# Transposing keys, queries and outputs by DMA from pair 8 on, in an attention and mixture-of-experts kernel on one core

## The chip, the cores and the metric

The kernel runs on one core of one Trainium2 chip. The metric is the device time of one execution in microseconds, as a median over runs. Engines are called as in the profile: PE is the matrix engine (PEld its weight loads), DVE the vector engine, ACT the scalar engine, POOL the GpSimd engine, and SP the engine that only issues DMAs and waits for them. A name with a q behind it (SPq, POOLq) is the engine's instruction queue. Every engine works through its own instructions in the order in which the program wrote them; between engines only semaphores order the work.

## The reference

Inputs are q, k and v of 4 batches, 8 heads, 768 positions and 64 elements, and the weights of a mixture of 8 experts (512 to 1024 to 512). The attention of one head, and then the experts on all 3072 rows:

```python
k_sum = k.reshape(B, H, nb, 32, D).max(axis=3)
v_sum = v.reshape(B, H, nb, 32, D).mean(axis=3)
scores_l = where(|pos_q - pos_k| < 16, scale * q @ k.T, -1e9)
scores_s = scale * q @ k_sum.T + log(32)
a = softmax(concatenate([scores_l, scores_s]))
attn = a @ concatenate([v, v_sum])            # heads are put side by side: x is 3072 x 512
P = exp(x @ w_gate - max); 8 times: P /= rows; P /= columns; P *= N / E
out = sum over e of P[:, e] * (relu(x @ w1[e]) @ w2[e])
```

## The kernel before, in words

**Pairs.** Two heads are worked on together. There are 16 such pairs, four to a batch, so that pair i belongs to batch i // 4. The four pairs of batch 0 are cut into two halves of 384 positions (pair_half); pairs 4 to 15 are taken whole (pair_whole). The steps of a whole pair, with the functions that do them, are:

- `load_qk`, `load_v` on POOL: two DMAs for k, two for q, one for v, cast from float32 to bfloat16 on the way, into the buffers kst, qst and vx. Each has six buffers (NQ), so the load of pair i waits until pair i - 6 has been read.
- The transposes of keys and queries. `tr` does them on PE, six 128x128 blocks for k and six for q, into a PSUM bank (tile tkq), and `tr_out` copies the bank to kT or qT on ACT or DVE. `tr_dma` does each with one DMA transpose from SP instead, from kst or qst straight into kT or qT. kT and qT have four buffers (NB): pair i overwrites those of pair i - 4 and has to wait for its last readers.
- `key_max` on DVE (lines 375 to 378, tiles kh, km, ksT): the largest key of each block of 32.
- `block_sums` on PE and `block_out` on DVE (tiles vs, Ve): the block means of v. `near_values`: four small DMAs from SP that put the rows at the edges of the 128-row tiles into Ve.
- `scores` on PE (tile sg), `score_exp` on ACT (er), `masks` (em) and `edges` (Ee) on DVE, `summaries` on PE (ss) and `summary_exp` on ACT, `values` on PE (av), `normalize` on DVE (rc, xs).
- The output's transpose into xT, the experts' input: `to_xT` on PE (six blocks, tile tx) with `x_out` as its copy on ACT or DVE, or `x_dma`, one DMA transpose from SP.

In the kernel before, pairs 4 to 11 have keys and queries transposed on PE and pairs 12 to 15 by DMA; outputs of pairs 10 to 14 go by DMA and the others on PE.

**The work beside it.** Expert 0 is done in plain form, half a batch (384 rows) at a time, while attention still runs: `hidden0` (tile hps, eight tiles of four matmuls each, one for each of the four pairs of the batch) and `project0` (tile yps, three row blocks in two parts). `expert0` of a batch needs the xT of that batch's four pairs. For the first half of batch 0 the first BEGUN = 2 hidden tiles are started with three of the four pairs, and the fourth matmul follows when its pair is there. After attention come experts 1 to 7 in a form with seven products instead of eight (lines 930 to 1125), 84 groups that repeat with a fixed period.

**Who sets the order.** Class Plan simulates all engines from costs and delays written in the code, and the instructions are emitted in the order of that simulation. A unit has an engine or several to choose from, a cost, dependences, a priority (smaller is more urgent; attention has 20 + i, expert 0 has 1000 and up) and a `lag`, the time that the plan allows after the unit's end before its readers can start, used for DMAs. At each step the plan takes, on each engine, the unit that could start first, and among those that could start within 0.02 us the most urgent one. Nothing is put in order again at run time: where the plan has put an instruction whose input comes late, its engine waits, and all that the plan put behind it waits too. The plan's PSUM banks are rings: three of tag m (expert 0), one double bank s (scores), three of tag a (the rest of attention).

`bridge` begins the second stage. It writes zeros into two PSUM banks with dummy matmuls (tile allg, three in the kernel before) and adds the row and column scalings of P to the plan.

Of the kernel before, what the change touches and what calls it, by code (L numbers as in the profile page):

```python
# [136 lines left out]
def kernel(  # L137
# [12 lines left out]
    B, H, S, D = q.shape  # L150
# [4 lines left out]
    KD = DM // 128  # L155
# [3 lines left out]
    PB = H // 2  # L159
# [76 lines left out]
    NB = PB  # L236
    NE = 2
    NS = 1
    NA = 3
    BEGUN = 2  # L240
    ctx.enter_context(tc.manual_schedule())
    first = ExitStack()
    wfirst = first.enter_context(tc.tile_pool(name="wfirst", bufs=1, side="right"))
# [4 lines left out]
    if True:  # L248
# [6 lines left out]
        kT = [attn.tile([128, S], BF16, name=f"kT{i}") for i in range(NB)]  # L255
# [318 lines left out]
                in_=at.pop(("lp", b)), func=AF.Exp, bias=0.0, scale=1.0 / XS)  # L574

        def hidden0(key, t0, f, dks):
            if f == 0 and 0 in dks:
                at["h", key] = hpool.tile([128, KF, HS], FP16, tag="h", name="h")
            if 0 in dks:
                at["hp", key, f] = bank("m", "hps")  # L580
            hidden_mm(0, at["hp", key, f], t0, HS, f, dks)
# [106 lines left out]
        def pair_start(i, prio):  # L688
            o = i - NB
            war_k = [U.get(("S", o, 0)), U.get(("S", o, 1)), U.get(("km", o))]  # L690
            war_q = war_k[:2] + [U.get(("ss", o, 0)), U.get(("ss", o, 1))]
            tag = "m" if i < PB else "a"
            for z in range(2 if i >= PB else 1):
                if i >= 12:
                    U["tr", i, z] = U["kT", i, z] = add("SP", 1.25, lambda z=z: tr_dma(i, z),
                                                        [U["kq"[z], i]] + (war_k, war_q)[z], prio, lag=5.5)
                    continue
                buf = Buffer(tag)
                U["tr", i, z] = add("PE", 0.5 if i < PB else 0.335, lambda z=z: tr(i, z, tag),
                                    [U["kq"[z], i], U["ident"]] + (war_k, war_q)[z]  # L700
                                    + [U["tr", i, 0] if z else U.get(("S", i - 1, 1 if i > PB else 0))],
                                    prio, opens=[buf], shape="col" if i < PB else None)
                U["kT", i, z] = add({"ACT": 0.8} if z == 0 else {"ACT": 0.8, "DVE": 0.95},
                                    0, lambda z=z: tr_out(U["kT", i, z].on, i, z), [U["tr", i, z]], prio,
                                    uses=[buf])
            if i < PB:
                query_half(i, 0, prio)
            U["km", i] = add("DVE", 0.85, lambda: key_max(i), [U["kT", i, 0]] + war_q[2:], prio)
            if i == 0:
                U["gc"] = add("DVE", 0.35, gate_constants, [U["km", 0]], 0.5)  # L710
            buf = Buffer("a")
            U["vs", i] = add("PE", 0.345, lambda: block_sums(i),
                             [U["v", i]] + ([U.get(("A", i - NE, 1))] if i >= PB else []), prio + 0.01, opens=[buf])
            U["Vs", i] = add("DVE", 0.24 if i < PB else 0.7, lambda: block_out(i), [U["vs", i]],
                             prio + 0.01, uses=[buf])
# [39 lines left out]

        def pair_whole(i, prio):
            U["near", i] = add("SP", 2.5, lambda: near_values(i), [U["v", i], U.get(("A", i - NE, 1))], prio,
                               lag=4.5)
            for h in range(2):
                buf = Buffer("s")  # L760
                U["S", i, h] = add("PE", 0.215, lambda h=h: scores(i, h),
                                   [U["kT", i, 0], U["kT", i, 1], U.get(("ed", i - 2))], prio, opens=[buf], shape="row")
                U["X", i, h] = add("ACT", 0.97, lambda h=h: score_exp(i, h), [U["S", i, h]], prio, uses=[buf])
                U["mk", i, h] = add("DVE", 0.56, lambda h=h: masks(i, h),
                                    [U["X", i, h], U.get(("A", i - 2, 1))], prio)
            U["ed", i] = add("DVE", 0.78, lambda: edges(i),
                             [U["X", i, 0], U["X", i, 1], U["mk", i, 1], U.get(("A", i - NE, 1))], prio)
            for h in range(2):
                buf = Buffer("a")
                U["ss", i, h] = add("PE", 0.17, lambda h=h: summaries(i, h, "a"),  # L770
                                    [U["km", i], U["kT", i, 1], U.get(("A", i - NE, 1))], prio, opens=[buf])
                U["sx", i, h] = add("ACT", 0.46, lambda h=h: summary_exp(i, h), [U["ss", i, h]], prio, uses=[buf])
            for h in range(2):
                buf = Buffer("a")
                U["A", i, h] = add("PE", 0.36, lambda h=h: values(i, h),
                                   [U["mk", i, h], U["ed", i], U["sx", i, h], U["Vs", i], U["near", i]],
                                   prio, opens=[buf])
                U["no", i, h] = add("DVE", 0.68, lambda h=h: normalize(i, h),
                                    [U["A", i, h], U.get(("xt", i - 2))], prio, uses=[buf])
            if 10 <= i < 15:  # L780
                U["xt", i] = U["x", i] = add("SP", 1.25, lambda: x_dma(i), [U["no", i, 0], U["no", i, 1]], prio,
                                             lag=6.5)
            else:
                buf = Buffer("a")
                U["xt", i] = add("PE", 0.34, lambda: to_xT(i), [U["no", i, 0], U["no", i, 1]], prio, opens=[buf])
                U["x", i] = add({"ACT": 0.8, "DVE": 0.9}, 0, lambda: x_out(U["x", i].on, i), [U["xt", i]], prio,
                                uses=[buf])

        halves, zero = [], []
# [1 line left out]
        def expert0(t0, xs):  # L791
            key, n = t0, len(halves)
            halves.append(key)
            pr = 1000.0 + n
            w = [U["w1", i] for i in range(2)]
            evac, old = [], [U.get(("pj", halves[n - 2], c)) for c in range(HG)] if n >= 2 else []
            for f in range(KF):
                buf = Buffer("m")

                k = KD - 1 if t0 == 0 and f < BEGUN else 0  # L800
                if k:
                    b = add("PE", 0.162 * k, lambda f=f, k=k: hidden0(key, t0, f, range(k)), xs[0:k] + [w[0]],
                            pr + f * 0.01, opens=[buf])
                    zero.append(b)
                m = U["hd", key, f] = add("PE", 0.65 - 0.162 * k, lambda f=f, k=k: hidden0(key, t0, f, range(k, KD)),
                                          xs + [w[f // 4]] + old + ([b] if k else []), pr + f * 0.01,
                                          **{"uses" if k else "opens": [buf]})

                def ev(f=f):
                    relu(U["rl", key, f].on, at["h", key][:, f, 0:HS], at.pop(("hp", key, f))[:, 0:HS])  # L810
                U["rl", key, f] = add({"ACT": 0.5, "DVE": 0.56}, 0, ev, [m], -1.0, uses=[buf])
                evac.append(U["rl", key, f])
                zero.extend([m, evac[-1]])
            for c in range(HG):
                buf = Buffer("m")
                p0 = add("PE", 0.866, lambda c=c: project0(key, c, 0), evac[0:4] + (U["w2d"] if t0 >= N // 2 else [U["w2"]]),
                         pr + 0.1 + c * 0.02, opens=[buf])
                p1 = add("PE", 0.866, lambda c=c: project0(key, c, 1), evac[4:8] + [p0],
                         pr + 0.11 + c * 0.02, uses=[buf])
                U["pj", key, c] = p1  # L820

                def ev(c=c):
                    copy(U["yo", key, c].on, out_acc[:, t0 // 128 + c, :], at.pop(("yp", key, c))[:])
                U["yo", key, c] = add({"ACT": 0.58, "DVE": 0.68}, 0, ev, [p1], -1.0, uses=[buf])
                zero.extend([p0, p1, U["yo", key, c]])
# [55 lines left out]
                expert0(b * S, xs)  # L881
                expert0(b * S + HS, xs)
        def hold():
            for r in range(12 % NB, NB):
                nc.gpsimd.tensor_copy(out=held[0:1, 0:1], in_=qT[r][0:1, W:W + 1])

        def hold_near():
# [27 lines left out]
    if True:  # L915
# [253 lines left out]

        def bridge():  # L1170
            t = [fps.tile([128, 512], FP32, tag="g", name="allg", bufs=2) for _ in range(2)]
            for n in (0, 1, 0):
                nc.tensor.matmul(t[n][:], lhsT=zeros[:], rhs=zeros[:, None, :].to_broadcast([128, 4, 128]),
                                 start=True, stop=True)
            plan.more({"ab": 2, "g": 2, "k": 1, "c5": 1, "c2": 1})
# [194 lines left out]
```

## Time and profile before

| what | value |
|---|---|
| median of 3 runs | 670.95 us (670.42 to 671.23) |
| the profiled execution | 669.62 us |
| its span, first to last instruction | 667.9 us |
| mean granted clock of PE | 0.999 |
| busy shares PE, PEld, DVE, ACT, POOL | 99%, 65%, 87%, 60%, 20% |
| DMA transposes: xT, kT, qT | 5, 4, 4 |
| PE matmuls of 128x128 transposes: tkq of whole pairs, tx | 96, 66 |

Rows of the groups give busy time and the mean duration of one instruction. The ends of matmuls are modelled and matmuls overlap, so what one more matmul costs PE is read from the distance between the starts of neighbours, not from the duration. A DMA's row on a queue is its issue; its landing is told apart. Attention lies in the first 115 us, expert 0 ends at about 164 us, and the 84 groups take the rest.

### The profile page before, as it was taken

To read this page: it belongs to the slowest core of one execution; us is meant where nothing else is said; L and a number is where in the kernel's file an instruction comes from. 1 tells how busy PE (TensorE), PEld (TensorE's weight loads), DVE (VectorE), ACT (ScalarE), POOL (GpSimd) and SP (SyncE) were. 2 spreads that over 40 slices of the span, in tenths; PEclk is the share of its full clock that TensorE was granted. 3 is DMA by queue.
4 is the path that set the end of the run, shared out by engine and by line. 5 is a ranking of instruction groups with operands and counts; after the bars stand their busy time and mean duration, and the time that the engine had idled before them with its cause. 6 is when DMAs were issued, how large, how long until landed. Compare 5 with 4: busy or idle time off the path is not lost.

```text
span 667.9 us, 13518 instructions
## 1 busy us (share of the span) xinstructions
PE 659.0 (99%) x5077; PEld 435.7 (65%) x5077; DVE 582.2 (87%) x1475; ACT 399.7 (60%) x782; POOL 131.8 (20%) x179
## 2 busy tenths in 40 slices
PE   8999999999999999999999999999999999999996
PEld 4766656555666666666666666666666666666665
DVE  8889998785999988998799978998899889998885
ACT  6777676566777765555555555555555555555551
POOL 8699404223011010201010000101020101100001
PEclk9999999999999999999999999999999999999999
DMA  9999939500513050503231051306040233201224
GB/s 162 184 154 147 148 72 95 71 1 8 73 17 32 1 80 1 49 1 55 26 33 17 0 80 17 33 1 79 1 47 3 39 41 29 20 1 64 79 80 158
DMA packets 124033, 36.75 MB, mean 55 GB/s; under 512 B 110144, under 2 KB 121152, under 8 KB 123968
## 3 DMA queue, kind: packets, MB, share of 16 engines
q0 software_dynamic: 104128, 25.93, 41.2%
q1 hardware_dynamic: 18880, 9.22, 6.1%
q8 instruction: 40, 0.66, 0.4%
q10 hardware_dynamic: 960, 0.74, 0.3%
q14 instruction: 25, 0.20, 0.1%
HBM read 52.45 MB, written 6.29 MB: 88 GB/s over the span
## 4 chain that ended last, share of the span: by engine, by line
PE 89%; DVE 7%; DMA 1%; ACT 1%; issue 1%; ACTq 0%; DVEq 0%
PE xy L989 37%; PE pg L983 16%; PE pa L983 11%; PE pb L983 11%; PE yps L231 5%; PE hps L221 5%; DVE xs L547 1%; DMA kT<-kst 1%; PE sg L383 1%; PE tkq L349 1%; DVE em L435 1%; DVE km L377 1%; DVE h L214 0%; DVE kh L375 0%; PE tx L554 0%
## 5 line engine op out<-in xcount | busy, mean ns | idle before, releaser
L989 PEld LDWEIGHTS <-hf 128*128 128x128 f16 x2352 | 230.1, 98 | 95.8 <-issue 0.8
L989 PE MATMUL xy<-w,hf 128*128 128x256 f16 x1312 | 183.4, 273 | 0.0
L989 PE MATMUL xy<-ws,hf 128*128 128x256 f16 x984 | 147.6, 273 | 0.1
L212 ACT ACTIVATE hf<-pg 128x512 f16<-128x512 f32 x84 | 50.1, 597 | 151.3 <-PE pg L983 151.2
L1125 DVE SCALAR_TENSOR_TENSOR out_acc<-xy,P_sb,out_acc 128x512 f32<-128x512 f32 x164 | 115.1, 744 | 2.1 <-PE xy L989 2.1
L930 DVE TENSOR_TENSOR hf<-hf 128x512 f16<-128x512 f16 x252 | 100.3, 425 | 8.9 <-DVE hf L933 0.5
L983 PE MATMUL pa<-xT,w 128*128 128x512 f16 x336 | 99.9, 379 | 0.0
L983 PEld LDWEIGHTS <-w 128*128 128x128 f16 x672 | 65.8, 98 | 43.5
L933 DVE TENSOR_TENSOR hf<-pb,c 128x512 f16<-128x512 f32 x84 | 58.1, 692 | 36.7 <-PE pb L983 34.4
L197 POOL DMA_DIRECT2D w<-in_moe_w_dram x56 | 41.8, 758 | 219.9 <-PE pg L983 191.7
L983 PEld LDWEIGHTS <-ws 128*128 128x128 f16 x504 | 49.3, 98 | 25.1
L1017 ACT COPY c<-pg 128x512 f32<-128x512 f32 x84 | 49.2, 585 | 22.4 <-PE pg L983 22.4
L933 DVE TENSOR_TENSOR hf<-pg,c 128x512 f16<-128x512 f32 x84 | 57.1, 680 | 0.7 <-PE pg L983 0.7
L212 ACT ACTIVATE hf<-pa 128x512 f16<-128x512 f32 x84 | 50.6, 603 | 0.9 <-PE pa L983 0.9
L1002 ACT COPY pg<-pa 128x512 f32<-128x512 f32 x84 | 47.9, 570 | 4.9
L983 PE MATMUL pg<-xT,w 128*128 128x512 f16 x168 | 50.0, 379 | 0.0
L983 PE MATMUL pg<-xTs,w 128*128 128x512 f16 x168 | 50.0, 379 | 0.0
L983 PE MATMUL pb<-xTs,ws 128*128 128x512 f16 x168 | 50.0, 379 | 0.0
L983 PE MATMUL pb<-xT,ws 128*128 128x512 f16 x168 | 50.0, 379 | 0.0
L983 PE MATMUL pg<-xTs,ws 128*128 128x512 f16 x168 | 50.0, 379 | 0.0
L1010 ACT COPY c<-pb 128x512 f32<-128x512 f32 x84 | 49.8, 593 | 0.0
L221 PE MATMUL hps<-xT,w 128*128 128x384 f16 x256 | 48.9, 326 | 0.0
(152 smaller groups left out, 827.5 us busy)
## 6 DMA issues: line engine op xcount, KB each, us to landing
w<-in_moe_w_dram POOLq DMA_DIRECT2D x8, 1024.0 KB, 9.0
w<-in_moe_w_dram POOLq DMA_DIRECT2D x56, 128.0 KB, 3.5
out_dram<-out_acc SPq DMA_DIRECT2D x20, 256.0 KB, 2.0
vx<-in_v_dram POOLq DMA_DIRECT2D x16, 192.0 KB, 5.9
qst<-in_q_dram POOLq DMA_DIRECT2D x31, 96.0 KB, 5.2
kst<-in_k_dram POOLq DMA_DIRECT2D x24, 96.0 KB, 5.4
w<-in_moe_w_dram POOLq DMA_DIRECT2D x2, 512.0 KB, 8.8
Ve<-vx SPq DMA_DIRECT2D x48, 10.2 KB, 4.0
```

The source lines that it names most:

```text
L197: nc.gpsimd.dma_start(out=t[:, :, h, :], in_=moe_w1[e].rearrange("(dk p) f -> p dk f", p=128)[:, :, f:f + 128])
L212: nc.scalar.activation(out=out, in_=in_, func=AF.Relu, bias=0.0, scale=1.0)
L221: nc.tensor.matmul(hp[:, 0:n], lhsT=w1s[e][:, dk, 128 * f:128 * (f + 1)], rhs=xT[:, dk, t0:t0 + n], start=(dk == 0), stop=(dk == KD - 1))
L231: nc.tensor.matmul(yp[:], lhsT=h[:, f, c * 128:(c + 1) * 128], rhs=w2s[e][:, f, :], start=(f == 0), stop=(f == KF - 1))
L930: nc.vector.tensor_tensor(out=out, in0=in0, in1=in1, op=ALU.subtract)
L933: nc.vector.tensor_tensor(out=out, in0=in0, in1=in1, op=ALU.add)
L983: nc.tensor.matmul(bank[:], lhsT=w[:, dk, :], rhs=x[:, dk, :], start=start and dk == 0, stop=dk == KH - 1, skip_group_check=True)
L989: nc.tensor.matmul(bank, lhsT=a(f)[:, 128 * c:128 * (c + 1)], rhs=w[:, f, :], start=start and f == 0, stop=f == FH - 1, skip_group_check=True)
L1002: nc.scalar.copy(out=B["g"][:], in_=B["a"][:])
L1010: nc.scalar.copy(out=B["c5"][:], in_=B["b"][:])
L1017: nc.scalar.copy(out=B["c2"][:], in_=B["g"][:])
L1125: nc.vector.scalar_tensor_tensor(out=acc, in0=src, scalar=P_sb[:, t, e:e + 1], in1=acc, op0=ALU.mult, op1=ALU.add)
```

## The change

Two constants are new, QKD = 8 and XD = 8: keys and queries are transposed by DMA from pair 8 on (12 before), and outputs of pairs 8 to 14 (10 to 14 before). The plan's delays for these DMAs and for the small DMAs of `near_values` now depend on the pair, and the plan's cost of a copy from PSUM by DVE is 0.57 us instead of 0.95 and 0.9; the copy of a whole pair's kT may now go to DVE as well. The first two hidden tiles of batch 1 are begun with three pairs, as those of batch 0 are, and the tile h is taken when the last of the four matmuls is written. `bridge` writes two dummy matmuls. `hold` reads the same four qT buffers as before, since 12 % NB is 0.

```diff
+    QKD = 8
+    XD = 8
...
         def hidden0(key, t0, f, dks):
-            if f == 0 and 0 in dks:
+            if KD - 1 in dks and ("h", key) not in at:
                 at["h", key] = hpool.tile([128, KF, HS], FP16, tag="h", name="h")
...
-                if i >= 12:
+                if i >= QKD:
                     U["tr", i, z] = U["kT", i, z] = add("SP", 1.25, lambda z=z: tr_dma(i, z),
-                                                        [U["kq"[z], i]] + (war_k, war_q)[z], prio, lag=5.5)
+                                                        [U["kq"[z], i]] + (war_k, war_q)[z], prio, lag=6.0 if i < 14 else 3.0)
                     continue
...
-                U["kT", i, z] = add({"ACT": 0.8} if z == 0 else {"ACT": 0.8, "DVE": 0.95},
+                U["kT", i, z] = add({"ACT": 0.8} if i < PB else {"ACT": 0.8, "DVE": 0.57},
                                     0, lambda z=z: tr_out(U["kT", i, z].on, i, z), [U["tr", i, z]], prio,
                                     uses=[buf])
...
             U["near", i] = add("SP", 2.5, lambda: near_values(i), [U["v", i], U.get(("A", i - NE, 1))], prio,
-                               lag=4.5)
+                               lag=4.5 if i < 13 else 3.0)
...
-            if 10 <= i < 15:
+            if XD <= i < 15:
                 U["xt", i] = U["x", i] = add("SP", 1.25, lambda: x_dma(i), [U["no", i, 0], U["no", i, 1]], prio,
-                                             lag=6.5)
+                                             lag=3.0 if 9 < i < 13 else 6.5)
             else:
                 buf = Buffer("a")
                 U["xt", i] = add("PE", 0.34, lambda: to_xT(i), [U["no", i, 0], U["no", i, 1]], prio, opens=[buf])
-                U["x", i] = add({"ACT": 0.8, "DVE": 0.9}, 0, lambda: x_out(U["x", i].on, i), [U["xt", i]], prio,
+                U["x", i] = add({"ACT": 0.8, "DVE": 0.57}, 0, lambda: x_out(U["x", i].on, i), [U["xt", i]], prio,
                                 uses=[buf])
...
-                k = KD - 1 if t0 == 0 and f < BEGUN else 0
+                k = KD - 1 if t0 in (0, S) and f < BEGUN else 0
...
-            for r in range(12 % NB, NB):
+            for r in range(NB):
                 nc.gpsimd.tensor_copy(out=held[0:1, 0:1], in_=qT[r][0:1, W:W + 1])
...
-            for n in (0, 1, 0):
+            for n in range(2):
                 nc.tensor.matmul(t[n][:], lhsT=zeros[:], rhs=zeros[:, None, :].to_broadcast([128, 4, 128]),
                                  start=True, stop=True)
```

## The prediction

> **What bounds the kernel now.** I read the page first (busy shares), then the engines' busy time by stretch, then the timeline of the pairs that change, then the DMA landings and the waits.
>
> ```profile
> PE 659.0 (99%) x5077; PEld 435.7 (65%) x5077; DVE 582.2 (87%) x1475; ACT 399.7 (60%) x782; POOL 131.8 (20%) x179
> ```
>
> ```profile
> core 0: us, PE busy (x) PEld busy (x) DVE busy (x) ACT busy (x) POOL busy (x), PEclk, DMA share, GB/s
> 25.00:45.00 20.00, 20.00 (x269) 13.54 (x268) 16.11 (x51) 14.99 (x27) 16.23 (x20) 1.00 2.26 159
> 45.00:65.00 20.00, 19.63 (x233) 13.05 (x231) 18.24 (x55) 14.04 (x23) 19.88 (x25) 1.00 2.28 149
> 65.00:85.00 20.00, 19.97 (x230) 12.79 (x228) 18.30 (x57) 14.30 (x25) 9.91 (x13) 1.00 1.87 143
> 85.00:105.00 20.00, 19.49 (x194) 11.00 (x193) 18.87 (x60) 14.85 (x26) 0.87 (x3) 1.00 0.35 66
> ```
>
> From 25 us to the end PE has work at nearly every moment, at the full clock; in 45 to 105 us it idles 0.37 + 0.03 + 0.51 = 0.91 us. Attention is not the bound: where it waits, PE does expert 0, of which some 49 us are left when attention ends at 115 us. So the time is the sum of PE's work, and work taken off PE shortens it, as long as PE never has to wait in its fixed order. DVE stands at 91 to 94% in 45 to 105 us and sets attention's pace. The DMA share of about 2.3 means that more than two packets per engine are in flight until 85 us.
>
> **What is removed.** PE's timeline shows pair 8's transposes and the matmuls behind them:
>
> ```profile
> 60.06 0.50 PE L349 MATMUL tkq<-ident,kst 128*128 128x128 bf16 x6
> 60.40 0.50 PE L349 MATMUL tkq<-ident,qst 128*128 128x128 bf16 x6
> 60.73 0.51 PE L393 MATMUL vs<-vx,m_blk 128*128 128x128 bf16 x6
> ```
>
> From start to start six blocks take 0.34 and 0.33 us, so 0.335; the durations of 0.50 overlap the neighbour. Eight such units go (pairs 8 to 11, at 60.06, 60.40, 64.63, 64.97, 71.38, 74.11, 81.57 and 81.91): 8 x 0.335 = 2.68 us. Two output transposes go (pair 8 at 71.83, next start 72.16; pair 9 at 80.01, next start 80.55, of which about 0.2 is a stall): 2 x 0.335 = 0.67 us. One dummy of 512 columns goes: three of 379 ns cover 0.8 us together, so a further one costs (0.81 - 0.38) / 2 = 0.216 us. It lies behind attention, where PE is full. The sum is 2.68 + 0.67 + 0.22 = 3.57 us.
>
> The Trainium skill ("VectorE: DVE Perf Modes", Rules for kernel authors) speaks against the change: a 128x128 transpose belongs on TensorE where PSUM is a fit destination, and on the DMA crossbar otherwise. Its table there gives 390 ns on TensorE and 1309 ns by DMA; by those the 60 blocks would free 23.4 us of PE (an estimate from that page), while the starts above show 56 ns for a block in a row of blocks, so the trace decides for 3.57.
>
> Off PE, the copies of these banks go: DVE copied qT of pairs 8 to 11 (0.55 us each, 2.2 us), ACT copied the four kT and two xT (0.80 each, 4.8 us). That is worth nothing in itself, but DVE is nearly full there, so attention can run up to 2.2 us ahead.
>
> **What is added.** Ten DMA transposes from SP.
>
> ```profile
> L354 SPq DMA_TRANSPOSE kT<-kst x4: 1210/1224/1323, 65.5 to 88.8; - x4
> L354 SPq DMA_TRANSPOSE qT<-qst x4: 1214/1243/1923, 67.7 to 90.2; - x4
> DMA to landing us min/median/max: 2.7/5.4/7.4
> ```
>
> *On SP*: ten issues of 1.24 us, 12.4 us in 46 to 85 us, beside 2.5 us for a pair's four small DMAs. That is about 5.0 us a pair (6.2 with the output) against a pair's pace of 6 to 7 us: it fits, but behind a transpose that waits for its load stand the small DMAs of the next pair, and `values` waits for those.
>
> *Landing*: 2.7 us when the DMAs are quiet, 7.0 to 7.4 us beside loads (pairs 12 and 13). The plan allows 1.25 + 6.0 = 7.25. They are issued early: k and q of pair 8 are loaded at about 46 and 47 us, so kT of pair 8 can land at about 54 us, while PE's route gave it at 61.4 us (copy at 60.60 + 0.80). The reuse of kst by the load of pair 14 (issued at 65.7) is still after that. The outputs of pairs 8 and 9 would be issued at about 71.8 and 80.3 us, when their `normalize` ends, and by the dearest row have landed by 79.2 and 87.7; the first to wait for that, `normalize` of pairs 10 and 11, came at 84.26 and 91.65.
>
> *On the DMA engines*: in the backlog after the w2 load v of pairs 4 and 5 landed at 32.50 and 36.33, so the five loads of a pair took 3.83 us, against 4.25 us between issues on POOL, so there is a spare tenth. A transpose occupies all engines for about 1.4 us when alone. Four pairs times 2.8 us plus two outputs are some 14 us more in a stretch that has little room; loads of pairs 10 to 13 will land 3 to 8 us later than the plan believes, which counts no DMA time for transposes.
>
> *The wait*: `key_max` on DVE is the first reader, and the plan puts it where it thinks the keys land, not where they are needed. This is shown already, for pair 12, whose scores come only at 88.5 us:
>
> ```profile
> 72.95 0.36 DVE L375 TENSOR_TENSOR kh<-kT 128x384 bf16<-128x384 bf16 x1 [0.71 <-DMA kT<-kst]
> ```
>
> DVE stood 0.71 us there with masks, normalisations and copies behind it, and PE lost almost nothing (0.03 us idle in that whole 20 us stretch). For the new stalls of PE I bound from below by -0.9 us (all of today's idle in 45 to 105 us vanishes) and from above by +6 us (DVE waits out most of an 8 us lateness, with some cover). I take +0.5, nearest to the row of pair 12.
>
> The two begun tiles: six matmuls of hps are moved, not added (162 ns each from start to start, 0.97 us). They matter at 61.9 to 65.9 us. There PE has run out of batch 0's expert work and batch 1 waits for pair 7's output (copied at 64.42 to 65.22); 1.34 us of the removed transposes lay just there, as filling. The begun tiles and pair 8's scores, ready earlier, take their place. If both failed, 1.34 us would be given back. The same gap threatens at 104 us, when batch 2 starts: pair 11's output lands at 97.50, but the plan believed 94.77 + 1.25 + 6.5 = 102.5. With a lag of 3.0 it is 99.0, so that end is loosened as far as PE moves up.
>
> **The sum.** The profiled span 667.9 - 3.57 + 0.5 = 664.8 us; with the 1.7 us around it 666.5, against 669.62, so -3.07. The median of the runs stands 1.33 us above the profiled execution: 670.95 - 3.07 = 667.9 us. About 0.2% (1.3 us) is what a measurement can tell from no change.
>
> **Rivals.**
>
> *Late keys stop DVE (slower).* The lateness grows with each pair, and DVE's order holds `key_max` of pairs 9 to 12 early. Loads of pair 10 would be some 3 us late, pair 11's 5 to 7. A DVE that waits 6 us in all, with 0.3 to 0.7 us of it covered each time, leaves some 5 us on PE, which ends 670.95 - 3.6 + 5 = 672.4 us. It decides from the point where the uncovered waits pass 3.6 + 1.3 = 4.9 us. For it: SP, POOL (19.88 of 20 us) and the DMAs are all full in 45 to 65 us, and the order is fixed. Against it: kT of pair 8 has 7 us in hand, every pair's loads come well ahead of its scores, and a wait counts once, since later steps shift with it.
> The Trainium skill ("DMA: Bandwidth & Descriptors", Queues, rings and completion order) says each DMA engine takes turns between queues packet by packet, so SP's transposes would not stand behind POOL's whole backlog. The small SP DMAs at 70 to 72 us landed in 5.3 to 5.7 us while loads took 6.2 to 7.2, which agrees only in part.
>
> *The hole before batch 1 opens.* Pair 7 does not come sooner and 1.34 us stay idle at 62 to 66 us: 667.9 + 1.3 = 669.2 us.
>
> *Moved stalls eat the gain.* The plan's new copy costs shuffle DVE and ACT from pair 4 on, and small waits, each below 1 us, add to some 3.5 us: about 671 us. The 0.91 us of idle time in 60 us of today's order speaks against so many.
>
> *The change does not do what it says*: the counts of matmuls follow from the code alone, so I give this nothing.
>
> **Chances.** Forecast 0.57, hole 0.12, eaten gain 0.14, late keys 0.17. Faster by over 0.2%: 0.57 + 0.12 = 0.69; within: 0.14; slower: 0.17. Range: from 670.95 - 3.57 - 0.9 = 666.5, rounded down to 666.3, to 671.8, which takes in the eaten gain and leaves out most of the late keys.
>
> **What would show it.** The rows would have tkq of whole pairs x48 (24 from kst, 24 from qst), tx x54, eight DMA transposes each into kT and qT, seven into xT, allg x2. PE's idle in 45 to 105 us at 1.5 us or less, and the period of the 84 groups unchanged at 6.08 us (the chain of waits shows the same piece at 173.39, 179.47 and 185.55). The late keys would show as idle DVE time in front of kh, ended by the DMA kT<-kst, of several us, with PE idle behind it. I am wrong if PE's idle in 25 to 120 us grows by over 2 us, or if the part after 164 us changes its length.

## The result, and the profile after

| | before | after |
|---|---|---|
| median (lowest to highest), us | 670.68 (670.14 to 671.23) | 678.84 (677.89 to 679.61) |
| ratio, 95% interval | 1 | 1.0125 (1.0112 to 1.0138) |
| span of the profiled execution, us | 667.9 | 677.5 |
| start of the first matmul of the 84 groups (xy), us | 163.25 | 172.74 |
| from there to the end of the span, us | 504.7 | 504.7 |

The change makes the kernel 1.25% slower. All of it is lost before the 84 groups begin. The page's row of busy times, and then the engines' busy time by stretch:

```profile
PE 655.8 (97%) x5016; PEld 432.6 (64%) x5016; DVE 580.0 (86%) x1469; ACT 396.3 (58%) x778; POOL 130.9 (19%) x179
```

```profile
core 0: us, PE busy (x) PEld busy (x) DVE busy (x) ACT busy (x) POOL busy (x), PEclk, DMA share, GB/s
25.00:45.00 20.00, 20.00 (x283) 14.04 (x281) 17.15 (x57) 16.35 (x29) 15.10 (x18) 1.00 2.14 151
45.00:65.00 20.00, 19.43 (x223) 12.01 (x221) 18.27 (x55) 14.08 (x24) 17.58 (x21) 1.00 2.16 150
65.00:85.00 20.00, 13.63 (x149) 8.54 (x150) 14.24 (x47) 10.02 (x18) 10.22 (x12) 1.00 1.79 139
85.00:105.00 20.00, 14.72 (x156) 8.98 (x155) 12.22 (x38) 11.06 (x20) 3.20 (x6) 1.00 1.71 150
105.00:125.00 20.00, 18.95 (x177) 10.96 (x175) 15.00 (x49) 11.20 (x20) 7.92 (x15) 1.00 0.97 97
```

PE's work did fall, from 659.0 to 655.8 us. But PE now idles 0.57 + 6.37 + 5.28 + 1.05 = 13.27 us in 45 to 125 us, where it idled 0.91 before. 12.4 us more idle time less 3.2 us less work is 9.2 us, and the span grew by 9.6. DVE fell from 18.3 and 18.9 us to 14.2 and 12.2 in the two worst stretches, so it is not DVE's work that holds PE up. The last two columns tell where to look: in 85 to 105 us the DMA share rose from 0.35 to 1.71 and the rate from 66 to 150 GB/s. The DMA engines are now full up to about 105 us instead of 85.

What PE waits for stands in PE's rows for 25 to 130 us (busy time, mean ns, then the idle time in front of them and what ended it). Before:

```profile
L383 PE MATMUL sg<-qT,kT 64*128 64x160 bf16 (+1 forms) x160 | 9.9, 231 | 0.0
L464 PE MATMUL av<-Ve,Ee 128*128 128x130 bf16 x72 | 8.1, 220 | 0.0
```

And after:

```profile
L385 PE MATMUL sg<-qT,kT 64*128 64x160 bf16 (+1 forms) x160 | 9.9, 230 | 8.7 <-DMA qT<-qst 8.7
L466 PE MATMUL av<-Ve,Ee 128*128 128x130 bf16 x72 | 8.2, 220 | 3.7 <-DMA Ve<-vx 2.4 <-DVE kh L378 1.2
L351 PE MATMUL tkq<-ident,kst 128*128 128x128 bf16 x24 | 2.0, 219 | 0.0
L351 PE MATMUL tkq<-ident,qst 128*128 128x128 bf16 x24 | 2.0, 219 | 0.0
L1175 PE MATMUL allg<-zeros 128*128 128x512 bf16 x2 | 0.6, 379 | 0.0
```

8.7 us are `scores` waiting for queries that a DMA transposes; 2.4 are `values` waiting for the small DMAs of `near_values`; 1.2 hang on `key_max`, late itself. DVE waits only 2.7 us in front of `key_max` (tile kh) for kT, and 3.6 us in `normalize` until an output's transpose has read xs. The other rows answer to the counts that the prediction named. PE's timeline shows a wait in front of nearly every pair's scores:

```profile
66.86 0.38 PE L385 MATMUL sg<-qT,kT 64*128 64x160 bf16 x6 [2.01 <-DMA qT<-qst]
79.46 0.38 PE L385 MATMUL sg<-qT,kT 64*128 64x160 bf16 x6 [2.50 <-DMA qT<-qst]
97.06 0.40 PE L466 MATMUL av<-Ve,Ee 128*128 128x130 bf16 x3 [2.42 <-DMA Ve<-vx]
101.31 0.38 PE L385 MATMUL sg<-qT,kT 64*128 64x160 bf16 x6 [1.85 <-DMA qT<-qst]
```

Last, the DMA issues of 40 to 105 us (KB each, then the median us from issue to landing), before:

```profile
kst<-in_k_dram POOLq DMA_DIRECT2D x16, 96.0 KB, 4.9
Ve<-vx SPq DMA_DIRECT2D x40, 10.2 KB, 3.7
qT<-qst SPq DMA_TRANSPOSE x4, 5.1
xT<-xs SPq DMA_TRANSPOSE x4, 2.8
```

and after:

```profile
kst<-in_k_dram POOLq DMA_DIRECT2D x16, 96.0 KB, 10.3
Ve<-vx SPq DMA_DIRECT2D x35, 10.2 KB, 6.1
qT<-qst SPq DMA_TRANSPOSE x7, 8.8
xT<-xs SPq DMA_TRANSPOSE x5, 7.6
```

Everything that goes by DMA takes 1.6 to 2.7 times as long, loads, small DMAs and transposes alike. Pair by pair the lateness grows. Class Plan's own times, by which it orders the instructions, had qT of pairs 9, 10, 11, 12 and 13 landed at 63.8, 66.3, 71.7, 78.4 and 88.4 us; in the trace they landed at 66.7, 71.4, 79.3, 87.2 and 101.3, so 3, 5, 8, 9 and 13 us late.

### The profile page after: what moved, and what is told of

Read it like the earlier page. It is cut to its first block, busy times and chain, and to the rows that moved or that the text cites. A ratio compares the mean times of both kernels' runs of the same rounds, so it can differ in the third digit from the quotient of the medians.

```text
span 677.5 us, 13407 instructions
## 1 busy us (share of the span) xinstructions
PE 655.8 (97%) x5016; PEld 432.6 (64%) x5016; DVE 580.0 (86%) x1469; ACT 396.3 (58%) x778; POOL 130.9 (19%) x179
## 4 chain that ended last, share of the span: by engine, by line
PE 84%; DMA 8%; DVE 3%; POOL 2%; issue 1%; SPq 1%; ACT 0%; DVEq 0%; POOLq 0%; ACTq 0%
PE xy L991 37%; PE pg L985 16%; PE pb L985 11%; PE pa L985 11%; PE hps L221 4%; PE yps L231 3%; DMA vx<-in_v_dram 3%; DMA qst<-in_q_dram 2%; DMA kst<-in_k_dram 2%; DMA kT<-kst 1%; POOL qst L296 1%; POOL kst L296 1%; POOL vx L320 1%; DMA qT<-qst 0%; PE py L991 0%
```

## The experiments

The theory after the comparison (called A in the expectations): the DMA engines' time adds up over loads and transposes. A pair in the stretch of the change needs 3.83 us for its loads, 2 x 1.4 for its transposes and 1.4 for its output, 8.0 us (an estimate). By bytes it comes out alike: its loads (576 KB) and three transposes (0.2 MB each) are 1.18 MB, 8.1 us at the 146 GB/s that the DMAs moved on average in 40 to 105 us. The plan sees none of the 4.2 us of transposes and has the queries of pairs 9 to 13 land 6.1 us apart on average (63.8 to 88.4). In the trace they landed 8.6 us apart (66.7 to 101.3), pairs 10, 11 and 12 at 71.43, 79.32 and 87.24. That is 2.5 us more a pair, and so the lateness grows from 3 to 13 us in four steps. The rivals were that the plan's hurry and order alone do it, that the number of packets of the loads does it, and that a DMA transpose is slow in itself.

Each ratio below is to the kernel before, run again beside the experiment; the change stands at 1.0125. In the edits, three dots mark what is left out.

**Which part of the change costs.** Three kernels take parts of it back.

`xd10`, outputs of pairs 8 and 9 again on PE:

```diff
-    XD = 8
+    XD = 10
```

> The changed kernel with the outputs of pairs 8 and 9 back on PE; the keys and queries of pairs 8 to 11 stay with the DMA. Theory A (the DMA engines are full and the plan counts no DMA time for a transpose, so the scores of pairs 8 to 15 stand on PE ahead of queries that land up to 14 us late): two of ten added transposes go, so most of PE's 13 us of idle time stays, 10 to 13 us, and the time is 675 to 680 us. Rival B (the output transposes are what hurts, since normalize waits for them and SP's order puts them ahead of others): below 672 us. Rival C (it is the new copy costs, delays and begun tiles that put the order wrong): unchanged, 678 to 680 us.

Measured 681.71 us, ratio 1.0178 (1.0162 to 1.0194): slower than the kernel after, though it has two DMA transposes less, and above the 675 to 680 that A gave. PE idles 0.42, 3.80, 7.15 and 1.73 us in the four stretches from 45 to 125, 13.1 in all, as after, and its granted clock is 0.91 in 85 to 105 us (1.00 in the kernel after). Two of 23 transposes were not what held it. It is slower by PE's busy time, 658.2 against 655.8 us: 0.67 are the two outputs' transposes on PE, and the rest agrees with the lower clock, which comes around its longest wait (3.96 us for qT, at 94 us).

`qkd12`, keys and queries of pairs 8 to 11 again on PE, outputs still by DMA from pair 8:

```diff
-    QKD = 8
+    QKD = 12
```

> The changed kernel with keys and queries of pairs 8 to 11 back on PE; outputs of pairs 8 and 9 stay with the DMA. Theory A: eight of ten added transposes go, PE has 2.7 us more work than in the changed kernel and idles 1 to 4 us in 25 to 125 us: 669 to 673 us. Rival B (outputs): above 675 us. Rival C (costs, delays, begun tiles): above 675 us.

Measured 671.99 us, ratio 1.0036 (1.0017 to 1.0054). Most of the loss is gone, and so the eight transposes of keys and queries carry it. What is left is one wait of 2.93 us in front of `values` at 99.3 us, for the small DMAs Ve<-vx, and a granted clock of 0.91 in that stretch.

`rest`, both limits back (12 and 10), only the plan's new costs and delays, the begun tiles and the missing dummy kept:

```diff
-    QKD = 8
-    XD = 8
+    QKD = 12
+    XD = 10
```

> The changed kernel with both limits back at 12 and 10, so that the copy costs, the delays, the begun tiles and the dummy matmul are all that is left of the change. Theory A: within 1.5 us of the kernel before (669 to 672 us), queries of pairs 12 to 15 a little late since the plan hurries. Rival C: 675 us or more.

Measured 670.88 against 670.03 us, ratio 1.0013 (1.0004 to 1.0022): the other edits together win nothing, and cost at most 0.2%.

**Transposes that nobody reads.** `scratch` is the kernel before, orders and costs of the plan unchanged, with eight DMA transposes more: keys and queries of pairs 8 to 11 are transposed on PE as before and by DMA once more, into rows of the output's buffer that nobody reads at that time.

```diff
         def tr(i, z, tag):
...
+            if i >= 8:
+                scr = out_acc[:, 18 + i % 4, 0:S // 2] if z else out_acc[:, 22 + i % 2, 0:S // 2]
+                nc.sync.dma_start_transpose(out=scr.bitcast(BF16).rearrange("c (g t) -> c g t", g=G),
+                                            in_=st[:].rearrange("p g j d -> p (g j d)"))
```

> The kernel before, in its own order, with eight DMA transposes more: k and q of pairs 8 to 11 are also transposed by DMA, into rows of out_acc that nothing has written yet, and nobody reads the result. PE does its transposes as before. It prices the DMA time alone. Theory A: loads of pairs 12 to 15 and the eight real transposes land several us later, 3 to 10 us of PE idle time, 672 to 680 us. Rival E (DMA time is to be had, and the changed kernel loses only since its plan hurries attention by 8 us and puts scores before their queries): within 1.5 us of the kernel before, 669 to 672 us.

Measured 677.67 us, ratio 1.0107 (1.0092 to 1.0122): the transposes cost 7.4 us though nobody reads what they produce, and though the order is that of before. The plan's hurry is therefore not needed for the loss. Three lines of its waits show the way it takes here (us in total, times, longest):

```profile
DVE kh L379 <- DMA kT<-kst: 6.1, 1, 6.1
PE yps L231 <- DVE h L214: 5.2, 1, 5.2
POOL kst L294 <- DMA out_acc<-kst: 3.5, 2, 2.8
```

kT of pair 12 lands at 79.14 us instead of 72.92. Its issue starts 4.1 us later, behind four extra transposes on SP's queue (69.62 instead of 65.54), and its row on SP lasts 4.2 us instead of 1.3; from the end of that row it lands in 5.3 us, no slower than the 6.1 of before. DVE waits 6.1 us for it in front of `key_max`, and 5.2 us of that reach PE. PE's busy time on the page grows by 1.6 us as well (660.6 against 659.0): the granted clock is 0.91 in 65 to 85 us. POOL's loads wait, too, until an added transpose has read kst (3.5 us) or qst (0.7). So `scratch` prices a transpose with its issue on SP and the buffer that it holds, and not DMA time alone; `half_loads` and `half_tr` below tell these apart.

**How many fit.** `before_qkd10` and `before_qkd14` are the kernel before with its limit of 12 moved:

```diff
-                if i >= 12:
+                if i >= 10:
```

> The kernel before with its limit for keys and queries at 10 instead of 12 and nothing else: four DMA transposes more, 1.34 us of PE work less. Theory A: the DMA engines have 5.6 us more to do in a full stretch and the plan does not know: PE idles 1 to 5 us more, 670 to 675 us. If transposes by DMA were free: 668.7 us. Rival C (the other edits): 668.7 us.

Measured 671.99 against 670.27 us, ratio 1.0024 (1.0010 to 1.0038): four transposes more by DMA lose a little, although four units of transposes (4 x 0.335 = 1.34 us) are gone from PE; its busy time on the page stays at 659.1 all the same, and it idles 0.27 + 0.39 + 1.93 = 2.59 us in 45 to 105.

```diff
-                if i >= 12:
+                if i >= 14:
```

> The kernel before with its limit 14 in place of 12: keys and queries of pairs 12 and 13 go back to PE, four DMA transposes less and 4 x 0.335 = 1.34 us more work on PE. Theory A: in the kernel before the DMA transposes of pairs 12 to 15 fit beside the loads (PE idle 0.91 us in 45 to 105), so nothing is won back and PE's work shows: 671.2 to 672.0 us. Rival H (the kernel before also pays for its DMA transposes, by waits of less than 1 us each, and the best limit lies above 12): 669.9 us or less.

Measured 670.36 against 670.04 us, ratio 1.0005 (0.9996 to 1.0015), no difference. The theory's 671.2 to 672.0 was a miss, and so was the rival's 669.9. PE's work grew by 1.3 us (660.3 against 659.0) and its idle time in 45 to 125 fell from 0.91 to 0.67; the first xy came 1.16 us later (164.41), as it should, but the span grew only by 0.6 us, so some half of it came back in the last 504 us, from where is open. The time is flat between limits of 12 and 14 and a little worse at 10. A limit of 8 was run only with the other edits in place (`xd10`, ratio 1.0178); these cost at most 0.2% in `rest`, so most of that step would belong to pairs 8 and 9 (argued, not run).

**Packets or bytes.** `long_rows` is the kernel after, but the loads of k and q of pairs 8 to 15 take runs of six rows (1536 bytes) to a partition instead of one row; it transposes the positions in another order than the reference wants. A load has 128 descriptors instead of 768 and the same bytes.

```diff
                 for j in range(2):
+                    if i >= 8:
+                        nc.gpsimd.dma_start(out=t[:].rearrange("p g j d -> p (g j d)")[:, j * G * D:(j + 1) * G * D],
+                                            in_=src[b, h0 + j].rearrange("(p g) d -> p (g d)", g=G))
+                        continue
```

> The changed kernel, same order, same ten added transposes, same bytes; but k and q of pairs 8 to 15 are loaded as one contiguous run of 1536 bytes for each partition (128 descriptors a DMA) instead of six runs of 256 (768 descriptors). The rows of keys and queries then stand in another order than the reference's, so its output differs; the work is the same. Theory A (the loads' packets fill the DMA engines and make the transposes late): landings of transposes fall from 7 to 10 us to 3 to 5, PE's idle time in 25 to 125 us from 13 us to 1 to 5, time 667 to 672 us. Rival D (transposes are slow in themselves or held by SP's own order): PE's idle time stays above 10 us, time above 676 us.

Measured 680.71 us, ratio 1.0154 (1.0138 to 1.0169), not better. The DMA page of 50 to 90 us, after and then `long_rows`:

```profile
DMA packets 36756, 5.75 MB, mean 144 GB/s; under 512 B 36753, under 2 KB 36753, under 8 KB 36753
```

```profile
DMA packets 23497, 5.94 MB, mean 149 GB/s; under 512 B 20427, under 2 KB 23494, under 8 KB 23494
```

A third of the packets less at about the same rate, and PE waits no less for qT (9.7 us against 8.7). A had put the price on the packets here and given 667 to 672 us, which was a miss. The number of packets is not the price, and from here on A means the time of the bytes.

`half_loads` is the kernel after with half the bytes: the loads of k and q of pairs 10 to 15 bring the first 384 positions, the other half of the buffer keeps older data.

```diff
-                t = attn.tile([128, G, 2, D], BF16, tag=nm, name=nm, bufs=NQ)
+                t = at["ld", i, z] = at["ld", i - NQ, z] if i >= PB + NQ else attn.tile(...)
...
-                    nc.gpsimd.dma_start(out=t[:, :, j, :],
-                                        in_=src[b, h0 + j].rearrange("(g p) d -> p g d", p=128))
+                    n = G if i < PB + NQ else G // 2
+                    nc.gpsimd.dma_start(out=t[:, 0:n, j, :],
+                                        in_=src[b, h0 + j, 0:n * 128].rearrange("(g p) d -> p g d", p=128))
```

> The kernel after, but the loads of k and q of pairs 10 to 15 bring only the first 384 of the 768 positions (the rest of the buffer keeps the data of six pairs before). Same number of DMAs, same order, same transposes; half the bytes and half the packets of twelve pairs of loads. Theory A (the DMA engines' time is additive: loads and transposes share it, and lateness is demand over pace): a pair's five loads took 3.83 us, so some 1.5 us a pair or 9 us in all are freed, the transposes of pairs 10 to 13 land in 4 to 7 us instead of 8 to 10, PE's idle time in 25 to 125 us falls from 13.3 to 3 to 6 us, and the time from 678.8 to 669 to 672 us. Rival G (a DMA transpose beside any load is slow in itself, or SP issues too slowly): landings stay at 7 to 10 us, idle time at 11 us or more, time 676 us or more.

`half_tr` leaves the loads whole and transposes three of six blocks of keys and queries of pairs 10 to 15.

```diff
-            nc.sync.dma_start_transpose(out=(kT[r][:], qT[r][:, W:W + S])[z].rearrange("c (g t) -> c g t", g=G),
-                                        in_=st[:].rearrange("p g j d -> p (g j d)"))
+            n = G if i < PB + NQ else G // 2
+            nc.sync.dma_start_transpose(out=(kT[r][:], qT[r][:, W:W + S])[z].rearrange("c (g t) -> c g t", g=G)[:, 0:n],
+                                        in_=st[:].rearrange("p g j d -> p (g j d)")[:, 0:128 * n])
```

> The kernel after, but the DMA transposes of k and q of pairs 10 to 15 do three of the six 128x128 blocks (the other half of kT and qT keeps the data of four pairs before). Loads, order and number of DMAs are as in the kernel after. Theory A (additive DMA time): twelve transposes save 0.7 us each, 8.4 us, nearly as much as the halved loads: idle time 3 to 6 us, time 669 to 673 us. Rival G (a transpose has a price that does not hang on its size, by its issue on SP or by its queue): landings stay at 7 us or more and the time at 676 us or more.

Measured 672.72 us, ratio 1.0039 (1.0026 to 1.0052), and 671.89 us, ratio 1.0029 (1.0018 to 1.0040). Two quite different cuts, each of 1.18 MB, some 8 us at 146 GB/s, bring back 0.86 and 0.96 of the 1.25% that the change lost, some 6 us each. Both keep every issue on SP and the order. The stretches of `half_tr` answer to those of the kernel after:

```profile
45.00:65.00 20.00, 19.34 (x223) 11.95 (x220) 18.26 (x55) 14.09 (x24) 17.80 (x21) 1.00 2.05 145
65.00:85.00 20.00, 16.94 (x173) 10.04 (x174) 16.88 (x56) 12.90 (x24) 12.23 (x15) 1.00 1.99 146
85.00:105.00 20.00, 17.63 (x191) 10.50 (x188) 14.22 (x44) 11.35 (x22) 0.35 (x2) 1.00 1.05 106
105.00:125.00 20.00, 19.92 (x172) 11.94 (x173) 16.35 (x54) 11.32 (x22) 9.86 (x17) 1.00 1.06 127
```

PE idles 0.66 + 3.06 + 2.37 + 0.08 = 6.17 us (6.82 in `half_loads`), just above the 3 to 6 expected, and the time of `half_loads` is just above its 669 to 672. In `half_loads` the transposes themselves were left whole, and these two rows of 40 to 105 us show them faster:

```profile
kT<-kst SPq DMA_TRANSPOSE x8, 5.2
qT<-qst SPq DMA_TRANSPOSE x8, 6.1
```

In the kernel after these were 8.4 and 8.8 us. In `half_tr` the halved transposes still took 7.1 and 6.7 us, close to the 7 that the rival gave as its sign, but the time came out far below its 676. So a transpose is not slow in itself. Loads and transposes spend one budget of DMA time, and either may be cut.

**Telling the plan.** In `plan_dma` every DMA transpose is charged 1.45 us on the plan's DMA engine and lands 0.4 us after that, as loads do; the small DMAs are charged 0.3 and 1.7.

```diff
+        def landed(us, lag, issued):
+            return add("LAND", 0, None, [add("DMA", us, None, [issued])], lag=lag)
...
-                    U["tr", i, z] = U["kT", i, z] = add("SP", 1.25, ..., prio, lag=6.0 if i < 14 else 3.0)
+                    U["tr", i, z] = U["kT", i, z] = landed(1.45, 0.4, add("SP", 1.25, ..., prio))
...
-            U["near", i] = add("SP", 2.5, ..., prio, lag=4.5 if i < 13 else 3.0)
+            U["near", i] = landed(0.3, 1.7, add("SP", 2.5, ..., prio))
...
-                U["xt", i] = U["x", i] = add("SP", 1.25, ..., prio, lag=3.0 if 9 < i < 13 else 6.5)
+                U["xt", i] = U["x", i] = landed(1.45, 0.4, add("SP", 1.25, ..., prio))
```

> The changed kernel, all ten transposes still by DMA, but the plan is told of them: each takes 1.45 us of the plan's one DMA server behind its 1.25 us of issue (0.3 us for the four small DMAs of a pair), in turn with the loads, and then 0.4 us (1.7 us) to land, in place of the fixed delays. Attention then ends at 126 us in the plan instead of 111. Theory A: PE does expert 0 while the queries are on their way, its idle time in 25 to 125 us falls from 13 us to below 3, and the time is 666 to 670 us. Rival D (the transposes by DMA are too slow in themselves, whatever the order: too little other work, or SP's own queue): still above 674 us.

Measured 684.29 us, ratio 1.0215 (1.0193 to 1.0237): slower still, and A's 666 to 670 was a plain miss. In 25 to 125 us PE idles 5.6 us instead of 13.3, so more than half of the waits there did go, though A gave under 3. But 1.48 us of idle time come in 125 to 145 us, and 5.47 in a stretch where the kernels before and after have none:

```profile
165.00:185.00 20.00, 14.53 (x71) 8.31 (x69) 12.11 (x28) 6.85 (x13) 5.70 (x8) 0.74 0.43 61
```

```profile
L1196 PE MATMUL sink<-csum_sb,col_en 128*128 128x8 f32 x8 | 1.8, 293 | 5.2 <-DVE csum_sb L1191 5.2
```

Those rows are the scalings of P: eight rounds, each of a few dependent steps on POOL, DVE and PE. They start when the last logits are there, and take 41 us (41 to 42 in the kernels before, after and `rest`). Here the logits are there at 134.4 us, so the chain's last step starts at 175.6, while the last matmuls of expert 0 start at 168.25. That was tested by `plan_dma_chain5`, the same kernel with five of the eight rounds (another P than the reference's):

```diff
-            for n in range(8):
+            for n in (0, 1, 2, 3, 7):
```

> The kernel whose plan counts the transposes' DMA time (684 us measured), with five of the eight rounds of row and column scaling left out down to five (its output is not the reference's). Theory F: with the plan told, half of its loss is a second wall: attention ends 13 us later than before, the eight scaling rounds take 40 us after it, expert 0's work is used up at 168 us and PE waits for the scaling until 175 us, then runs at a lower clock for some us. With three rounds (15 us) less this wait is gone and the time is 674 to 677 us. Rival G (the later end of attention costs nothing, the loss is all idle time inside attention): 682 us or more.

Measured 676.76 us, ratio 1.0090 (1.0073 to 1.0107), 7.5 us less than `plan_dma`:

```profile
165.00:185.00 20.00, 20.00 (x128) 12.38 (x127) 17.45 (x35) 13.35 (x27) 2.44 (x3) 1.00 0.48 67
```

PE is full there again. So an honest plan does not save the change: the time that the DMA engines need is then taken at the end, from the cover of the scaling chain. And with that wait gone the kernel is still 0.9% slower than before: PE idles 7.0 us between 25 and 145 us, and the granted clock is 0.91 in two of these stretches.

No run beat the kernel before; `before_qkd14` equals it.

## Why the prediction was wrong, point by point

- **Removed work, 3.57 us: right.** The rows show tkq x24 + x24, allg x2, and PE's busy time fell by 3.2 us. The part behind the first xy kept its length (504.7 us). The hole at 62 to 66 us did not open: PE idled 0.57 us in 45 to 65 us.
- **New stalls, +0.5 us with 6 as the upper end: wrong, and this is the term that failed.** It measured +12.4 us. The row of pair 12 in the kernel before, on which the value was set, belongs to a time when the loads were about to end (DMA full up to 85 us). It was not a price for four pairs before it. The prediction's own sign of being wrong, PE's idle time up by over 2 us, came six times over.
- **"A spare tenth" and 14 us of DMA work more: the sum was not made.** 14 us of work into the 39 us from 46 to 85, of which a tenth is free, are 10 us of lateness, and the runs with some 8 us less of DMA work got some 6 us back. The 1.4 us for a transpose "when alone" holds beside loads and not alone: at 146 GB/s its 0.2 MB take 1.35 us, while alone the trace of before has them pass at 203 to 226 GB/s, in 0.9 to 1.0 us (both estimates). The prediction had the lateness of the loads at 3 to 8 us, but let it fall on PE once, reduced by cover.
- **"A wait counts once, since later steps shift with it": wrong.** That holds for one late transfer. Here demand (8.0 us a pair) exceeded pace, so each pair was later against the plan than the last (3, 5, 8, 9, 13 us), and nearly every pair brought a wait of its own.
- **"A pair's pace of 6 to 7 us": the wrong pace.** It was read from the trace of before. The new plan, with less on DVE and no DMA time for transposes, starts the scores of pairs 8 to 12 5.0 us apart (59.3 to 79.3 us in its own times) where the plan before had 6.4 (63.3 to 89.0); over pairs 8 to 15 it is 5.6 against 5.8. That was the very thing that the prediction welcomed ("attention can run up to 2.2 us ahead"). SP did not fit either: in the kernel after the issue of a transpose took up to 3.2 us, with a median of 1.6 for kT, against 1.24 in the sum.
- **Landing at 7.4 us at most: too low.** The median was 8.1 and 8.5 us for kT and qT, the longest 10.3. Outputs of pairs 8 and 9 landed at 85.4 and 91.3 us instead of by 79.2 and 87.7. The lag of 3.0 for outputs of pairs 10 to 12, meant to loosen the start of batch 2, allowed 4.25 us where pair 10 took 8.7.
- **The rival of late keys: right in cause, wrong in place and price.** The wait fell on PE, for qT in front of `scores` (8.7 us), and only 2.7 us on DVE for kT. In `scratch`, where the order was that of before, it came just as the rival said, 6.1 us on DVE and 5.2 behind it on PE.
- **"Where it waits, PE does expert 0, of which some 49 us are left": not slack.** The scaling chain needs 41 us after the last logits, and expert 0 is what PE does meanwhile. In the kernel before the chain's last step started at 161.4 us and expert 0's last matmul at 163.0, in the kernel after at 167.0 and 172.5: 1.6 and 5.5 us to spare, not 49. `plan_dma` used that up.
- **The rule of the Trainium skill ("DMA: Bandwidth & Descriptors", Queues, rings and completion order)** that engines take turns packet by packet was weighed as speaking against the rival. Turns did not keep transposes quick: those of keys and queries of pairs 8 to 13 landed in 6.6 to 10.3 us, and the loads of k beside them took a median of 10.3 us instead of 4.9. How the turns were shared no run shows. The other rule of the Trainium skill that was weighed ("VectorE: DVE Perf Modes", Rules for kernel authors), that a transpose belongs on TensorE where PSUM is a fit destination, came out right for pairs 8 to 11. What decided here was DMA time.

## What to carry to other kernels

Before work is moved onto an engine that is shared, DMA engines included, make the sum of demand against pace there for each step of the loop, with the pace that the new order will ask for; if demand is above pace, the lateness grows with every step, and the price is the whole excess rather than one wait. A planner's delay for a transfer does not say that the engine is taken: two transfers with a lag each seem to cost nothing together. And work that "is left over" behind a stage has to be checked for what it covers before it is spent.

## What the runs showed of the hardware

- Casting loads and transposes together moved 139 to 150 GB/s over the three stretches of 20 us from 45 to 105 us in the kernel after. Over the 40 us from 50 to 90 it was 144 GB/s there and 149 in `long_rows`, with 36756 and 23497 packets. Transposes alone moved 203 to 226 GB/s in the trace of before (around 90 us, where they land in 2.7 us).
- The granted clock of PE fell to 0.91 over 20 us in some kernels with waits of several us on PE (5.2 us in `scratch`, 4.0 in `xd10`, 3.1 in `long_rows`, 2.9 in `qkd12`), in `plan_dma` around two waits of 1.8 and 1.1 us close together, and to 0.74 where PE idled 5.5 us in `plan_dma`. But it stayed at 1.00 in the kernel after with 6.4 us of idle time in waits of up to 2.5 us, and in `half_loads` with one wait of 3.0 us. Length alone does not part them, and no run isolated it. In `scratch` PE's busy time was 1.6 us longer with it.
